# S4 convolution and MLP block on one core: the recorded order of 1,094 operations, the choice of engine and the PSUM slots replaced by another set

## The chip, the cores and the metric

One core of one Trainium2 chip runs the program. The core has five engines that work at the same time, each through its own list of instructions and strictly in that list's order: TensorE (PE in the profile; its weight loads are shown apart as PEld), VectorE (DVE), ScalarE (ACT), GpSimd (POOL) and SyncE (SP, which here only issues transfers). They meet through semaphores. Matmul results land in PSUM, which this kernel treats as eight slots (0 to 7) of 128 x 512 float32. The metric is the device time of one execution in microseconds (us).

## The reference

A layernorm, a long convolution whose kernel is a sum of 128 complex exponentials for each of 512 channels, a skip, then two layernorms, an MLP with GELU and another skip, on a 2048 x 512 input in bfloat16:

```python
def _A_ref(u, A_re, A_im, B_re, B_im, C_re, C_im, log_dt, Dskip):
    dt = jnp.exp(log_dt)[:, None]
    logdA = dt * (A_re + 1j * A_im)
    P = jnp.exp(logdA[:, :, None] * l[None, None, :])
    K = jnp.einsum("dn,dnl,dn->dl", Cc, P, dt * Bc).real
    ...
    return irfft(rfft(u, 2L) * rfft(K, 2L))[:L] + u * Dskip

def _B_ref(x, w1, b1, w2, b2):
    h = gelu(layernorm(x) @ w1 + b1)
    return h @ w2 + b2

h = x + _A_ref(layernorm(x), ...)
h2 = h + _B_ref(layernorm(h), ...)
```

## The kernel before

The program does not loop over tiles when it is built. It first writes down 1,094 operations, each with the engine or the two engines that may run it, what it reads and writes, and the PSUM slots that it needs. Then `Sched.run` goes through a recorded list, `ORDER`, and emits them in that order. An entry of 0 or more is twice the number of an operation, plus 1 if the second of its two engines is to run it; for a copy out of PSUM (`evac`) an even entry is ACT and an odd one DVE. A negative entry -1-z is a fill: one 128 x 128 x 512 matmul of the identity into the free slot z whose result nobody reads (L1434 in the profile). `SLOTS` says, digit by digit, in which slot each PSUM tile starts. An engine's own instructions are those of the list that belong to it, in the list's order, so `ORDER` sets each engine's queue, the order in which SP issues transfers, and with the slots who waits for whose PSUM tile. No time is computed when the program is built.

The 512 channels are handled in four blocks c = 0 to 3 of 128, in two halves (0 and 1, 2 and 3). The work around the change, in the order in which the data flow:

- Front (lines 560 to 760): small elementwise operations on DVE and ACT make rates, angles and sizes; 48 small transfers of 16 KB restack them (SP). `bexps` (L723) and `aexps` (PE L964, ACT L967) make the exponentials.
- `chain` (half; PE L992, ACT L1000, DVE L1010) and `chain1` (one block; PE L1024 and L1027, ACT L1029, DVE L1031): phases are added up in PSUM step by step, ACT takes the sine of each step, DVE multiplies it into the exponentials. The next step of a chain adds onto the PSUM tile that the sine reads, so it waits for that sine.
- `kgen` (block; PE L1054 and L1055, 512 pairs of narrow matmuls in all): the convolution kernel's table. It needs all five steps of the block's `chain1`. Operations 605 to 608, 610 and 611 are block 2, operations 628 to 634 block 3.
- `kspec` (blocks 0 and 1, L1084) and `kspec1` (block 2 or 3, L1109) put the table in order; it goes to DRAM (AK_d, AKc_d) and comes back transposed (KF). `fstage` (L940) is the second step of the transform; `austage` (L919) the first step for the input. `ktail` and `klate` (L1148, L1169) do the same for the late part. The copies out of PSUM of all of these are `evac` (ACT L517, DVE L519).
- The second half of the input's rows is loaded by eight transfers (`load_u(1)`), which wait for two tables made by ACT; DVE takes its statistics (L899) and normalises it (L906).
- `inverse` (DVE L1193, PE L1203): the products of spectra and the inverse transform, first for the first 1024 rows (operations 656 to 694), then for the others (846 to 897). Results are transposed by SP transfers (L1219), for block 3 of the first half on PE (L1212).
- `tail` (L1273, L1278 and the statistics of the layernorms) and `mlp` (PE L1321, ACT L1323 for the GELU, PE L1337, DVE L1339, output transfers). Operation 850 is the first matmul group of the inverse for the second 1024 rows; what PE has after it is the same in both orders but for the sequence.

Of the kernel before, what the change touches and what calls it, by code (L numbers as in the profile page):

```python
# [182 lines left out]
class VS(V):  # L183
# [60 lines left out]
SLOTS = "01012012034626026502020244602624062662062604046020262604064202462704264026024602460264206406204602467024602745020120415701425601624024672303642074350501246210675460165323401613712360172314231041502310"  # L244
# [5 lines left out]
class Sched:  # L250
# [44 lines left out]
    def run(self, nslots):  # L295
# [13 lines left out]
        taken = [None] * nslots  # L309
        given = iter(SLOTS)  # L310
        order, seen = [], set()
# [1174 lines left out]
```

## Time and profile before

| | |
|---|---|
| time, median of 3 runs | 245.29 us (243.12 to 245.49) |
| the profiled execution's own time | 245.59 us |
| its span in the profile | 243.2 us |
| PE busy | 215.4 us in 3,696 matmuls, 38 of them fills |
| DVE busy | 179.6 us in 407 instructions |
| ACT busy | 170.5 us in 232 instructions |
| transfers | 21.40 MB in 42,448 packets |

The span is the profile's time from the first to the last instruction; the difference of 2.4 us to the execution's own time lies around it. All engines run side by side, so busy times are no sum: in each stage the question is which queue is full, and what ended the last wait before it.

### The profile page before, as it was taken

How to read it: one execution, taken by the hardware profiler on the slowest of the kernel's cores; microseconds unless marked ns; L12 is line 12 of the kernel's file. 1: busy time of each engine (PE TensorE's matmuls, PEld its weight loads, DVE VectorE, ACT ScalarE, POOL GpSimd, SP SyncE). 2: the span in 40 equal slices, each digit the busy share in tenths (PEclk: the TensorE clock that was granted, in tenths of full speed). 3: DMA queues.
4: the chain of work that ended last, by engine and by line, in shares of the span. 5: the costliest groups of instructions: out<-in, count | busy, mean ns of one | idle time of the engine just before them, and what ended most of it. 6: DMA issues, size and time to landing. Idle time of an engine off the chain costs nothing.

```text
span 243.2 us, 8615 instructions
## 1 busy us (share of the span) xinstructions
PE 215.4 (89%) x3696; PEld 126.2 (52%) x3705; DVE 179.6 (74%) x407; ACT 170.5 (70%) x232; POOL 18.3 (8%) x145
## 2 busy tenths in 40 slices
PE   7559786878988876979998999999999999999994
PEld 2436243656634454755775476655554444444443
DVE  6999999999999995659998988797506991213022
ACT  3999999999999956975997987785134402903700
POOL 8800000011000000300000010010000101000000
PEclk9999999999999999999999999999999999999999
DMA  5121124000013943417899485644514051142303
GB/s 149 34 62 44 38 19 82 20 3 7 3 25 82 214 132 125 125 30 163 231 159 210 121 254 95 214 80 85 99 28 83 0 106 27 41 88 65 86 19 71
DMA packets 42448, 21.40 MB, mean 88 GB/s; under 512 B 30761, under 2 KB 40618, under 8 KB 42410
## 3 DMA queue, kind: packets, MB, share of 16 engines
q1 hardware_dynamic: 42250, 20.79, 38.0%
q8 instruction: 29, 0.48, 0.8%
q10 hardware_dynamic: 160, 0.07, 0.1%
q14 instruction: 9, 0.07, 0.1%
HBM read 10.33 MB, written 4.49 MB: 61 GB/s over the span
## 4 chain that ended last, share of the span: by engine, by line
PE 59%; DVE 26%; DMA 5%; issue 4%; SPq 3%; ACT 1%; DVEq 0%; ACTq 0%
PE ps L1321 16%; PE ps L1337 16%; PE ps L1203 7%; DVE ar L579 5%; DVE ar L519 4%; DMA ar<-ar 4%; PE ps L919 4%; PE ps L940 3%; DVE ar L1010 3%; SPq L530 3%; DVE ar L584 3%; PE ps L1054 3%; DVE ar L1031 3%; PE ps L1278 3%; PE ps L1055 2%
## 5 line engine op out<-in xcount | busy, mean ns | idle before, releaser
L517 ACT CAST ar<-ps 128x1024 bf16<-128x1024 f32 (+4 forms) x66 | 59.0, 941 | 16.7 <-PE ps L1203 7.5
L1323 ACT ACTIVATE ar<-ps,ar 128x512 bf16<-128x512 f32 (+1 forms) x44 | 27.6, 686 | 35.3 <-PE ps L1321 35.3
L1321 PE MATMUL ps<-ar 128*128 128x512 bf16 (+1 forms) x176 | 39.8, 379 | 0.0
L1337 PE MATMUL ps<-ar 128*128 128x512 bf16 (+2 forms) x179 | 38.5, 366 | 0.6 <-issue 0.3
L1339 DVE TENSOR_TENSOR ar<-ps,ar 128x512 bf16<-128x512 f32 (+1 forms) x17 | 10.8, 657 | 36.1 <-PE ps L1337 32.7
L519 DVE CAST ar<-ps 128x1024 bf16<-128x1024 f32 (+5 forms) x29 | 29.2, 1015 | 8.9 <-ACT ar L1029 2.8
L1193 DVE TENSOR_TENSOR ar<-ar 128x1024 bf16<-128x1024 bf16 x48 | 30.7, 685 | 6.5 <-PE ps L1203 6.0
L1337 PEld LDWEIGHTS <-ar 128*128 128x128 bf16 (+1 forms) x187 | 18.0, 98 | 19.6
L1321 PEld LDWEIGHTS <-ar 128*128 128x128 bf16 (+1 forms) x176 | 17.2, 100 | 20.4 <-issue 1.0
L1054 PE MATMUL ps<-ar 128*20 128x33 bf16 x512 | 20.0, 249 | 6.1 <-issue 5.6
L1203 PE MATMUL ps<-ar 64*128 64x128 bf16 x768 | 23.7, 216 | 0.1
L1203 PEld LDWEIGHTS <-ar 64*128 64x128 bf16 x768 | 21.5, 94 | 4.3 <-issue 2.1
L1029 ACT ACTIVATE ar<-ps 128x1024 bf16<-128x1024 int16 x20 | 19.6, 1039 | 3.0 <-issue 2.4
L579 POOL TENSOR_TENSOR ar<-ar 128x4 f32<-128x4 f32 (+1 forms) x6 | 7.4, 1226 | 187.5 <-DVE ar L584 149.3
L1010 DVE TENSOR_TENSOR ar<-ar 128x1024 bf16<-128x1024 bf16 x32 | 21.2, 684 | 0.2
L1055 PEld LDWEIGHTS <-ar 128*20 128x20 bf16 x512 | 17.7, 125 | 6.5 <-issue 6.4
L1055 PE MATMUL ps<-ar 128*20 128x33 bf16 x512 | 20.1, 248 | 0.0
L1054 PEld LDWEIGHTS <-ar 128*20 128x20 bf16 x512 | 17.6, 124 | 3.0 <-DVE ar L1031 1.5
L723 ACT ACTIVATE ar<-ar 128x512 bf16<-128x512 f32 x32 | 18.2, 628 | 0.5 <-DVE ar L565 0.5
L919 PE MATMUL ps<-ar 128*32 128x512 bf16 x256 | 15.7, 380 | 1.4 <-ACT ar L517 0.6
L1027 PE MATMUL ps<-ar 128*32 128x256 f16 (+2 forms) x288 | 13.5, 280 | 2.8 <-ACT ar L1029 2.7
L1031 DVE TENSOR_TENSOR ar<-ar 128x512 bf16<-128x512 bf16 x40 | 15.4, 413 | 0.3
(99 smaller groups left out, 284.6 us busy)
## 6 DMA issues: line engine op xcount, KB each, us to landing
ar<-in_A_u_dram SPq DMA_DIRECT2D x16, 128.0 KB
ar<-in_A_u_dram SPq DMA_DIRECT2D x8, 256.0 KB
out_dram<-ar SPq DMA_DIRECT2D x30, 64.0 KB
ar<-in_B_w_dram SPq DMA_DIRECT2D x4, 344.0 KB
ar<-in_B_w_dram SPq DMA_DIRECT2D x2, 640.0 KB
AK_d<-ar SPq DMA_DIRECT2D x2, 512.0 KB
ar<-AK_d SPq DMA_DIRECT2D x2, 512.0 KB
AKc_d<-ar SPq DMA_DIRECT2D x4, 256.0 KB
```

The lines of the kernel that those rows point to most:

```text
L517: act.copy(out_fn(), in_fn())
L519: dve.tensor_copy(out_fn(), in_fn())
L919: pe.matmul(pst(p)[32 * j:32 * j + 32, 512 * z:512 * z + 512], lhsT=BX.ap()[:, f0 + z, 16 - 16 * c:48 - 16 * c], rhs=src[2 * j + c].ap(), ...
L1010: add("DVE", c_dve(1024, 2), lambda e, lo=lo, rv=rv, sz=sc[z], e0=e0, o0=o0, q=q: dve.tensor_tensor(ent(o0, q, lo, 4, rv), ent(e0, q, lo, ...
L1031: add("DVE", c_dve(512, 2), lambda e, sc=sc, b0=b0, tb=tb, z=z: dve.tensor_tensor(tb[b0:b0 + 4].ap(), EA[c][b0:b0 + 4].ap(), sc[z].ap(), A ...
L1054: pe.matmul(o, lhsT=Ar.ap()[:, :, d], rhs=Br.ap()[:, :, d], start=True, stop=False, tile_position=(0, 32 * g))
L1055: pe.matmul(o, lhsT=Ai.ap()[:, :, d], rhs=Bi.ap()[:, :, d], start=False, stop=True, tile_position=(0, 32 * g))
L1193: dve.tensor_tensor(o, a, b_[:, :, ::-1, :] if sw else b_, ALU.mult)
L1203: pe.matmul(pst(p)[:, 512 * h + 128 * k:512 * h + 128 * k + 128], lhsT=q.ap()[rows, 2 * k + r, :], rhs=TP[w].ap()[rows, f0 // 2 + k, :], s ...
L1321: pe.matmul(pst(p)[:fs], lhsT=w1s[dc].ap()[:, fc * P:fc * P + fs], rhs=ybuf.ap().rearrange("p (t c) k -> p c t k", c=4)[:, dc], start=(dc ...
L1323: add("ACT", c_act(512, 1), lambda e, p=p, fc=fc, fs=fs: act.activation(hT.ap()[:fs, fc, :], pst(p)[:fs], ACT.Gelu_apprx_tanh, bias=b1_sb. ...
L1337: pe.matmul(pst(p)[:, c0:c1], lhsT=hT.ap()[:fs, fc, 128 * t:128 * t + 128], rhs=w2s[fc].ap()[:fs, c0:c1], start=(fc == 0), stop=(fc == NFC ...
```

## The change

The code stays as it is, line for line. `ORDER` and `SLOTS` are replaced. The same 1,094 operations are emitted; what differs:

- TensorE has 70 fills in place of 38. Between operation 532 (the first kgen group of block 0) and operation 605 (the first of block 2) there are 29 in place of 3; after operation 850 there are 9 in place of 10.
- Of the operations that either of ACT and DVE may run, 27 go from DVE to ACT and 24 from ACT to DVE, nearly all of them copies out of PSUM.
- PE: ahead of operation 605 it has six operations more: the austage group 422, the last three steps of chain1 for block 3 (494, 498, 502), the fstage group 572 and the small selection (530). In the old order these stand between the kgen groups of block 2 or later. Among the kgen groups of blocks 2 and 3 there now stand fstage groups and the two kspec1 groups of block 2.
- ACT: ahead of the last sine that kgen of block 2 needs (operation 483) seven copies and two sines (491, 495) come in, five copies go out. DVE: ahead of the last product that kgen of block 2 needs (485) seven copies and one product (496) come in, and two very small ones, five copies go out.
- SP: of the eight loads of the second half of the input, three stand ahead of the first AK_d write and one behind it; then a write of the late part, the second AK_d write, the other late write, the last four loads, and the two reads of AK_d. In the old order all eight loads stand ahead of both AK_d writes, with the two late writes among the two reads.
- The slots of most PSUM tiles differ.

The list's core around operation 605 (entry 1210):

```diff
 ORDER = [
...
-    770, 968, 970, 976, 774, 866, 863, 852, 1210, 982, 1212, 988, 854, 978, 844, 984, 760, 986, 990, 1214, 846, 996, 998, 1012, 772, 1114, 1140, 1142,
-    1014, 1106, 1216, 1004, 1218, 1024, 1020, 1220, 1026, 1006, 1016, 1022, 1160, 1000, 992, 1116, 1002, 1124, 1126, 994, 1144, 1163, 1222, 1120,
...
+    844, 864, 866, 972, 948, 784, 914, 840, 936, 974, 950, 980, 847, 944, 938, 946, 848, 956, 843, 982, 988, 856, 1208, 851, 958, 964, 952, 954, 960,
+    852, 990, 1106, 966, 859, 968, 996, 998, 1144, 962, 992, -1, -1, -1, 1004, 1006, 970, 1210, 1206, 774, 778, 780, 776, 1024, 1212, 1214, 854, 984,
...
 ]
-SLOTS = "01012012034626026502020244602624062662062604046020262604064202462704264026024602460264206406204602467024602745020120415701425601624024672303642074350501246210675460165323401613712360172314231041502310"
+SLOTS = "01201210213462462424024025260420620464646042402040460242640260424600002460426024204604202460260420462304206345600167246074120120462460230452362040615360730561047654354670170230124123145606567215210412"
```

More of the change, by code (lines that the diff above doesn't have):

```diff
@@ L199 @@
 ORDER = [
[43 rows of a table removed]
[44 rows of a table added]
 ]
-SLOTS = "01012012034626026502020244602624062662062604046020262604064202462704264026024602460264206406204602467024602745020120415701425601624024672303642074350501246210675460165323401613712360172314231041502310"
+SLOTS = "01201210213462462424024025260420620464646042402040460242640260424600002460426024604204602460260420462304206345600167246074120120462460230452362040615360730561047654354670170230124123145606567215210412"
 TURN = 450000
```

83 rows, old and new, of the table ORDER are left out of this document.

## The prediction

> **What bounds the kernel now.** I read the page first, for which engine is full in which part of the span.
>
> ```profile
> PE 215.4 (89%) x3696; PEld 126.2 (52%) x3705; DVE 179.6 (74%) x407; ACT 170.5 (70%) x232; POOL 18.3 (8%) x145
> PE   7559786878988876979998999999999999999994
> DVE  6999999999999995659998988797506991213022
> ACT  3999999999999956975997987785134402903700
> ```
>
> One slice is 6.1 us. For the first fifteen slices DVE and ACT are both full and PE is not; from slice 18 (about 109 us) PE is full to the end. The view of busy time by stretch, cut where PE starts the kgen groups of block 2 (85.2), kspec1 of block 3 (108.6) and operation 850 (139.06), says it in numbers:
>
> ```profile
> 46.00:62.00 16.00, 13.21 (x550) 10.78 (x547) 15.85 (x42) 15.97 (x28) 1.69 (x1) 1.00 0.03 7
> 62.00:85.20 23.20, 20.45 (x458) 10.84 (x456) 22.84 (x48) 23.18 (x28) 0.00 (x0) 1.00 0.42 86
> 85.20:108.60 23.40, 18.60 (x644) 13.92 (x644) 16.19 (x41) 17.07 (x20) 2.16 (x2) 1.00 0.36 106
> 108.60:139.06 30.46, 29.39 (x660) 18.51 (x662) 27.89 (x38) 25.91 (x30) 0.00 (x0) 1.00 0.81 171
> 139.06:239.90 100.84, 100.15 (x967) 53.94 (x973) 52.98 (x108) 47.34 (x69) 4.03 (x4) 1.00 0.39 87
> ```
>
> The columns are length, busy time of PE, PEld, DVE, ACT and POOL with instruction counts, granted clock, the transfers' share and GB/s. Up to 85.2 the two elementwise engines leave no gap (23.18 and 22.84 of 23.20). After 139.06 PE is busy for 100.15 of 100.84 us, and both orders have the same work there but for one fill. So the question is when operation 850 starts. The weak stretch is the third, where no engine is full: PE idles 4.8 of 23.4 us. The chain of waits names what it waited for:
>
> ```profile
> 82.50 0.44 PE ps L1027 x16
> 82.94 0.86 PE ps L919 x16
> 85.22 0.27 PE ps L1054 x4
> 85.48 0.07 PE ps L1055 x4
> ...
> 86.63 1.62 issue
> ...
> 91.13 0.55 PE ps L940 x4
> ...
> 92.34 1.83 issue
> ...
> 103.24 0.33 PE ps L1133 x4
> ...
> 105.72 1.01 issue
> ```
>
> "Issue" is a wait for nothing that the profile shows. The group of line 1054 in this stretch puts 4.5 us on it:
>
> ```profile
> L1054 PE MATMUL ps<-ar 128*20 128x33 bf16 x256 | 10.5, 249 | 4.5 <-issue 4.5
> ```
>
> These waits stand at fixed distances. Counted between the end of one and the start of the next:
>
> ```profile
> 46.70:50.20 3.50, 2.44 (x148) 2.32 (x137) 3.50 (x8) 3.49 (x9) 0.00 (x0) 1.00 0.05 10
> 88.20:92.30 4.10, 4.05 (x128) 2.81 (x128) 4.02 (x8) 3.00 (x4) 0.00 (x0) 1.00 0.71 200
> 94.10:105.60 11.50, 11.43 (x384) 8.69 (x384) 7.02 (x20) 10.06 (x12) 2.16 (x2) 1.00 0.29 85
> 106.70:130.50 23.80, 23.31 (x639) 16.51 (x638) 21.57 (x31) 17.98 (x22) 0.00 (x0) 1.00 0.80 161
> ```
>
> From 88.20 to 92.30 PE runs 128 matmuls and 128 loads, 256 instructions; from 94.10 to 105.60 it runs 768, three times 256; from 106.70 to the wait at 130.72 it runs 1,277, within the few records that a trace lacks five times 256. So PE stops where a block of 256 instructions ends and the next is not there. The view of transfers shows blocks on a queue of their own (q8, 16 KB a packet). Here are four windows: 82.1 to 85.7, 85.7 to 86.8, 86.8 to 91.8 and 91.8 to 93.
>
> ```profile
> q1 hardware_dynamic: 1909, 1.00, 115.6%
> ...
> q8 instruction: 1, 0.02, 5.2%
> ...
> q1 hardware_dynamic: 352, 0.63, 46.8%
> ...
> q8 instruction: 1, 0.02, 5.0%
> ```
>
> The first and third have no q8 packet at all: for 3.6 and 5.0 us the data queue had the engines, and PE's waits end at 88.25 and 94.17, 1.2 to 1.5 us after the windows that hold the next q8 packet. SP's own timeline says which data: eight input loads and two AK_d writes up to 81.6, then the AK_d reads.
>
> ```profile
> 74.05 1.87 SPq L530 DMA_DIRECT2D ar<-in_A_u_dram  x3
> 76.60 3.74 SPq L530 DMA_DIRECT2D ar<-in_A_u_dram  x5
> 80.44 1.16 SPq L530 DMA_DIRECT2D AK_d<-ar  x2
> 88.12 0.34 SPq L530 DMA_DIRECT2D ar<-AK_d  x1
> ```
>
> **A rule against the change.** The row: two waits of 1.62 and 1.83 us at block ends. The Trainium skill, Runtime: NRT & Kernel Launch, section on instruction fetch mechanics, states that instructions come in 16 KiB blocks of 256, fetched while the current one runs, and that crossing a block's end is mostly hidden. The trace agrees on the 256 and not on "hidden". By that rule the waits would have another cause, and spacing the instructions would save none of them; that is the second rival below.
>
> **The change part by part.**
>
> *The start of the kgen groups of block 2 moves later.* They need the last sine and product of that block's chain1. ACT has two sines and, net, two copies more ahead of that point; DVE net two copies and a product more. From the page:
>
> ```profile
> L517 ACT CAST ar<-ps 128x1024 bf16<-128x1024 f32 (+4 forms) x66 | 59.0, 941 | 16.7 <-PE ps L1203 7.5
> L519 DVE CAST ar<-ps 128x1024 bf16<-128x1024 f32 (+5 forms) x29 | 29.2, 1015 | 8.9 <-ACT ar L1029 2.8
> L1029 ACT ACTIVATE ar<-ps 128x1024 bf16<-128x1024 int16 x20 | 19.6, 1039 | 3.0 <-issue 2.4
> L1031 DVE TENSOR_TENSOR ar<-ar 128x512 bf16<-128x512 bf16 x40 | 15.4, 413 | 0.3
> ```
>
> Busy time by count is 0.98 per sine and 0.89 per copy on ACT, so 3.7 us; on DVE 1.01 per copy and 0.39 per product, so 2.4. Both queues were full, so nothing hides it. I take 3.3, near ACT's end since its window is the fuller, less something for two half-size copies: 88.5 in place of 85.2.
>
> *PE work is moved ahead of that start.* The austage group (0.86), three chain1 steps (0.44 each), an fstage group (0.55) and the selection (0.33) leave the stretch, 3.06 us. Four fills come in. The next rows are from the whole chain:
>
> ```profile
> 130.72 0.84 issue
> 141.36 2.26 PE ps L1434 x10
> ```
>
> A fill is 0.226 us, four are 0.9. Net -2.2 us. So the two first terms nearly cancel, and the gain has to come from the block waits.
>
> *The block waits.* Four kgen matmuls with their four loads take 0.07 us (the row at 85.48), so a block of nothing but kgen is used up in 256/8 x 0.07 = 2.2 us. With almost no transfers (the window 46.70 to 50.20, share 0.05) one block period took 3.5 us with PE idle for 1.06: that is the floor, and a wait of 1.3 us for a pure block. In the new order the run from 605 to the end of kgen of block 3 spans five blocks. The first is nearly pure (605 to 607) and the last about half as short (631 to 634 and four fills, 3.0 us); the middle ones hold thirteen fstage and kspec1 groups and last 3.8 us or more, over the floor. So at least 1.3 + 0.5 = 1.8 us stays. Whether more stays depends on transfers: the first AK_d write and half of the loads now go out earlier, and the AK_d reads no longer wait behind all eight loads, so they should be over when the run starts; but the loads of x for the tail (98 us in the old order) still fall into it. Bounds: 1.8 stay, or all 4.5. I take 2.3, near the floor: -2.2 us. Each block later has more work in it; of the wait at 130.72 I count half, -0.4, with 0 and -0.84 as its ends.
>
> *The second stretch and the end.* Copies that were deferred come back between 88 and 139. DVE, ACT and PE each have room there (16.2, 17.1 and 18.6 of 23.4 busy in the third window), so I cost them at nothing; if DVE fails to fit, its 2.4 us comes back. After 850 one fill less: -0.2. The table lookups and the front (two copies moved to ACT) are inside the first term, since ACT is counted from its start.
>
> Sum: +3.3 - 2.2 - 2.2 - 0.4 - 0.2 = -1.7. The profiled execution took 245.59 (span 243.2 and 2.4 around it), so 243.9. The median of the runs, 245.29, lies 0.3 below that execution, so 243.6.
>
> **The rivals.**
>
> *More is won.* The start moves by 2.4 only, the block waits fall to the floor (-2.7) and the one at 130.72 goes (-0.84): with -2.2 and -0.2 that is -3.5, and 241.8; less if the copies that waited for late sines (2.8 us in the L519 row) close up too, down to about 239. For it: no engine is full in the third window. Against it: DVE was busy for 27.89 of 30.46 in the fourth.
>
> *The waits stay as they are* (the rule above, or transfers that now meet the run in another place): +3.3 - 2.2 - 0.2 = +0.9, so 246.2. For it: a pure first block, requested just when the AK_d reads may still run. Against it: the 256-counts and the q8 packets.
>
> *Slower: PE becomes the bound ahead of the kgen run.* Between the first kgen groups and operation 605 PE gets 26 more fills (5.9 us) and the moved work (3.1), 9.0 us. It had idle time of 2.79 and 2.75 us in the first two windows, and the later start gives 3.3: 8.8. Nothing is left, while a step of a chain still has to wait for the sine ahead of it and holds up everything behind it on PE: the next step, and through it ACT and DVE. If all of the old idle time (5.5) was such waiting and is paid again, the time is 243.6 + 5.5 = 249.1. From 1.7 us of it on the kernel is slower than before, from 4.1 on by over 1%; I price it at 248. For it: the balance. Against it: a fill needs no data, so it can run early in a wait that is there anyway; then only its last 0.2 us can hold anything up.
>
> **How the numbers follow.** One per cent (2.45 us) is about what a measurement of this kernel tells from no change; the three runs differ by 2.4. Chances: the forecast (242.2 to 245.2) 0.42, more won 0.26, the waits stay 0.13, PE the bound 0.19. Faster by over 1% is under 242.84: 0.26 and 0.10 of the forecast's lower end, 0.36. Slower by over 1% is over 247.74: 0.17 of the last rival. The rest, 0.47, is within 1%. The range leaves out a tenth on each side: the far end of "more won" below 240.3 and PE as the bound in full above 248.3.
>
> **What would show it.** In the changed kernel's profile operation 605 should start near 88.5 us (first L1054 group of block 2) and 850 near 137.6 (the first L1203 group of 64 matmuls); the L1054 group should have 2 to 3 us on "issue" after 88 us, at distances of 256 instructions, and q8 packets no more than 1.5 us after a block's end. If ACT or DVE has gaps between 46 and 88 that end on PE L1027 or L992, PE has become the bound. If L1054 still has 4.5 us on issue, the spacing did nothing. If 850 starts before 136, the deferred copies cost less than I think.

## The result: 1.3 per cent slower, and the profile after

| | old order | new order |
|---|---|---|
| median of 18 runs each, side by side | 243.69 us (241.81 to 248.37) | 246.55 us (244.98 to 248.56) |
| ratio, 95% interval | | 1.0126 (1.0095 to 1.0158) |
| the profiled execution's own time, its span | 245.59 us, 243.2 | 245.81 us, 243.9 |

The ratio, here and below, compares runs of both orders made side by side and leaves out those more than 1.5 per cent above the fastest of their kernel, so it is not the quotient of the medians. The forecast was 243.6. The time is inside the range but on the other side of no change: a change of -1.7 us was forecast, and the medians differ by +2.9. The forecast started from 245.29, the median of three runs; the median of the 18 is 1.6 us lower. Note the table's last row: the two profiled executions differ by 0.2 us, the medians by 2.9. The execution of the old order that the prediction read was 1.9 us above the median of its kernel, that of the new order 0.7 below.

These are the page's rows for the new order (line numbers are one higher than in the old kernel):

```profile
PE 223.8 (92%) x3729; PEld 128.5 (53%) x3737; DVE 179.9 (74%) x404; ACT 171.7 (70%) x235; POOL 18.2 (7%) x145
...
PE   7559787989998999989999999999999999999993
...
DVE  6999999999899999778799889874525893003022
ACT  4899989989999979957789989695124516601900
...
L1055 PE MATMUL ps<-ar 128*20 128x33 bf16 x512 | 19.3, 249 | 1.1 <-issue 0.8
L1435 PE MATMUL ps<-ar 128*128 128x512 bf16 x70 | 18.0, 383 | 1.6 <-issue 1.2
```

PE has 8.4 us more of busy time, and 32 fills more (L1435, 18.0 us for 70, so 0.257 us each) are 8.2 of it. The kgen group L1055 (it was L1054) waits 0.8 us on issue. In the old profile it was 5.6 us, 4.5 of them in the kgen run of blocks 2 and 3:

```profile
L1054 PE MATMUL ps<-ar 128*20 128x33 bf16 x512 | 20.0, 249 | 6.1 <-issue 5.6
```

So most of the block waits of that profile are gone. The view of busy time by stretch says what was paid (columns as in the prediction; the borders are 605 at 91.33, 634 at 107.68 and 850 at 139.02):

```profile
46.00:62.00 16.00, 14.80 (x540) 11.24 (x538) 15.86 (x43) 15.05 (x26) 1.69 (x1) 1.00 0.10 12
62.00:75.00 13.00, 12.29 (x229) 5.64 (x231) 11.99 (x27) 12.97 (x16) 0.00 (x0) 1.00 0.06 12
75.00:91.33 16.33, 15.57 (x339) 8.46 (x331) 15.86 (x30) 14.75 (x18) 0.00 (x0) 1.00 0.85 205
91.33:107.68 16.35, 15.80 (x585) 12.61 (x585) 13.88 (x32) 13.99 (x16) 2.16 (x2) 1.00 0.31 78
107.68:139.02 31.34, 29.83 (x676) 18.33 (x668) 27.35 (x42) 25.38 (x30) 0.00 (x0) 1.00 0.88 186
139.02:240.04 101.02, 100.39 (x967) 53.72 (x972) 51.92 (x105) 48.93 (x72) 4.03 (x4) 1.00 0.38 77
```

In the first three rows PE idles only 2.7 of 45.3 us, and now ACT (15.05 of 16.00, 14.75 of 16.33) and DVE (11.99 of 13.00) have gaps that they did not have. Operation 605 starts 6.1 us later than in the old profile, not 3.3. The kgen run, from the start of 605 to the start of 634, is shorter, 16.35 in place of 21.53 us. Of the old order, the same view for that run and for what follows it:

```profile
85.22:106.75 21.53, 17.06 (x587) 12.79 (x589) 15.45 (x38) 16.68 (x19) 2.16 (x2) 1.00 0.39 114
106.75:139.06 32.31, 30.93 (x720) 19.64 (x721) 28.61 (x40) 26.27 (x31) 0.00 (x0) 1.00 0.77 162
```

Why 605 is late is read from the timeline of the new order (start and length in us):

```profile
51.73 1.02 PE L1435 MATMUL ps<-ar 128*128 128x512 bf16 x4 [1.17 <-issue]
52.69 0.62 PE L791 MATMUL ps<-ar 128*32 128x256 f16 x16
...
64.49 1.28 ACT L512 ACT_TABLE_LOAD   x1
...
65.64 1.32 DVE L520 CAST ar<-ps 128x726 bf16<-128x726 f32 x2 [0.61 <-PE ps L1056]
67.00 0.18 DVE L1069 TENSOR_TENSOR ar<-ar 128x32 bf16<-128x32 bf16 x1
67.09 0.88 DVE L585 SCALAR_TENSOR_TENSOR ar<-ar 128x256 f32<-128x256 f32 x2
...
69.11 5.85 SPq L531 DMA_DIRECT2D ar<-ar  x8
```

and of the old one:

```profile
61.82 1.28 ACT L511 ACT_TABLE_LOAD   x1
...
63.87 0.88 DVE L584 SCALAR_TENSOR_TENSOR ar<-ar 128x256 f32<-128x256 f32 x2
...
66.16 6.05 SPq L530 DMA_DIRECT2D ar<-ar  x8
```

This is one chain: the exponentials end, ACT loads the table for the sines (operation 357), ACT and DVE make the sizes for blocks 2 and 3 (358 to 363), SP restacks them in eight transfers, and only then does chain1 of block 2 start (466), five steps of which end in 605. In the new order five fills (the last four take 1.02 us) stand on PE ahead of the group at L791, and ACT waits 0.92 us for that group before it can copy its result out (operation 339, 53.36 us). This copy and a smaller one (104) were on DVE in the old order; now they stand in ACT's queue ahead of 357. On DVE two copies, the first of them after 0.61 us of waiting for PE, stand ahead of operation 359. Starts of the chain's members in several profiles, in us:

| operation | old, as read | old, 2nd profile | old, 3rd | new | new, 2nd | new, no fills | old, with fills |
|---|---|---|---|---|---|---|---|
| 357, table load (ACT) | 61.82 | 61.73 | 62.19 | 64.49 | 64.17 | 63.39 | 63.57 |
| restack (SP, first of 8) | 66.16 | 66.07 | 66.51 | 69.11 | 68.81 | 68.69 | 69.54 |
| 466, chain1 of block 2 | 73.19 | 73.09 | 73.63 | 76.49 | 76.08 | 76.48 | 77.28 |
| 483, its last sine | 83.06 | 82.96 | 83.41 | 88.23 | 87.92 | 87.61 | 86.83 |
| 485, its last product | 84.73 | 84.64 | 85.09 | 90.86 | 90.55 | 90.24 | 88.48 |
| 605, first kgen of block 2 | 85.22 | 85.12 | 85.57 | 91.33 | 91.03 | 90.71 | 88.96 |
| 634, last kgen of block 3 | 106.75 | 103.05 | 104.38 | 107.68 | 107.49 | 106.83 | 108.77 |
| 850 | 139.06 | 135.19 | 136.93 | 139.02 | 138.25 | 137.42 | 140.40 |
| run's own time | 245.59 | 241.39 | 243.40 | 245.81 | 245.13 | 244.23 | 247.46 |

### The profile page after: what moved, and what is told of

Same layout as the page of the kernel before. It is cut to its first block, busy times and chain, and to the rows that moved or that the text cites. A ratio compares the mean times of both kernels' runs of the same rounds, so it can differ in the third digit from the quotient of the medians.

```text
span 243.9 us, 8671 instructions
## 1 busy us (share of the span) xinstructions
PE 223.8 (92%) x3729; PEld 128.5 (53%) x3737; DVE 179.9 (74%) x404; ACT 171.7 (70%) x235; POOL 18.2 (7%) x145
## 4 chain that ended last, share of the span: by engine, by line
PE 63%; DVE 15%; ACT 13%; issue 4%; DMA 3%; SPq 0%; DVEq 0%; ACTq 0%
PE ps L1322 16%; PE ps L1338 15%; PE ps L1204 9%; DVE ar L1011 4%; ACT ar L518 4%; DVE ar L580 4%; PE ps L920 3%; PE ps L1435 3%; PE ps L941 3%; PE ps L1055 3%; ACT ar L1030 3%; PE ps L1279 2%; DVE ar L585 2%; PE ps L1056 2%; ACT ar L724 2%
## 5 line engine op out<-in xcount | busy, mean ns | idle before, releaser
L518 ACT CAST ar<-ps 128x1024 bf16<-128x1024 f32 (+3 forms) x66 | 58.5, 942 | 15.6 <-issue 4.9
L1194 DVE TENSOR_TENSOR ar<-ar 128x1024 bf16<-128x1024 bf16 x48 | 30.9, 686 | 8.5 <-PE ps L1204 6.7
L520 DVE CAST ar<-ps 128x1024 bf16<-128x1024 f32 (+4 forms) x29 | 29.0, 1013 | 7.2 <-issue 3.4
L1338 PEld LDWEIGHTS <-ar 128*128 128x128 bf16 (+1 forms) x187 | 18.1, 98 | 19.7
L1204 PE MATMUL ps<-ar 64*128 64x128 bf16 x768 | 24.2, 216 | 0.0
L1204 PEld LDWEIGHTS <-ar 64*128 64x128 bf16 x768 | 21.5, 94 | 4.7 <-issue 3.0
L1011 DVE TENSOR_TENSOR ar<-ar 128x1024 bf16<-128x1024 bf16 x32 | 20.3, 675 | 0.5 <-ACT ar L592 0.3
L1055 PE MATMUL ps<-ar 128*20 128x33 bf16 x512 | 19.3, 249 | 1.1 <-issue 0.8
L1435 PE MATMUL ps<-ar 128*128 128x512 bf16 x70 | 18.0, 383 | 1.6 <-issue 1.2
L1056 PE MATMUL ps<-ar 128*20 128x33 bf16 x512 | 19.3, 249 | 0.0
L1055 PEld LDWEIGHTS <-ar 128*20 128x20 bf16 x512 | 17.4, 124 | 3.4 <-issue 2.2
L1032 DVE TENSOR_TENSOR ar<-ar 128x512 bf16<-128x512 bf16 x40 | 15.9, 418 | 0.7 <-ACT ar L1030 0.3
```

The source lines that it names most:

```text
L518: act.copy(out_fn(), in_fn())
L520: dve.tensor_copy(out_fn(), in_fn())
L1011: add("DVE", c_dve(1024, 2), lambda e, lo=lo, rv=rv, sz=sc[z], e0=e0, o0=o0, q=q: dve.tensor_tensor(ent(o0, q, lo, 4, rv), ent(e0, q, lo, ...
L1055: pe.matmul(o, lhsT=Ar.ap()[:, :, d], rhs=Br.ap()[:, :, d], start=True, stop=False, tile_position=(0, 32 * g))
L1056: pe.matmul(o, lhsT=Ai.ap()[:, :, d], rhs=Bi.ap()[:, :, d], start=False, stop=True, tile_position=(0, 32 * g))
L1194: dve.tensor_tensor(o, a, b_[:, :, ::-1, :] if sw else b_, ALU.mult)
```

## The experiments

Times are medians; "ratio" is to the old order, run beside it on the same chip. Each diff shows the place that changed, taken out of longer lines of the list, and where several places change in the same way it shows one of them.

**before_again, before_third: the old order unchanged**, for other profiles of it.

> The kernel before, unchanged, profiled once more. Theory D (draw): the profiled execution of the kernel before that the prediction read, 245.59 us, was a slow draw; its median over 18 runs is 243.69. If its surplus of 1.9 us lay in the waits at the ends of instruction blocks, a second profile shows 1.5 to 2.5 us less on issue before line 1054 (it had 4.5) and operation 850 starts near 137 us in place of 139.06. Rival: the waits are the same in every execution (4.0 to 5.0 us), and the surplus lies elsewhere.

> The old order unchanged, a third profile. The landmarks up to 605 within 0.3 us of the first two (85.1 to 85.2); the run from 605 to 634 anywhere from 17.9 to 21.5 us, and operation 850 later or earlier with it (135.2 with the run of 17.9, 139.1 with 21.5). If it comes out near 18 again, the execution that the prediction read was the odd one.

242.54 us, ratio 0.9984 (0.9937 to 1.0031), and 243.20 us, ratio 0.9997 (0.9965 to 1.0029). The page's kgen group in the second and in the third profile:

```profile
L1054 PE MATMUL ps<-ar 128*20 128x33 bf16 x512 | 19.5, 249 | 2.3 <-issue 2.0
```

```profile
L1054 PE MATMUL ps<-ar 128*20 128x33 bf16 x512 | 19.6, 249 | 2.8 <-issue 2.3
```

The table's front is the same within 0.5 us in all three, but the run from 605 to 634 took 21.5, 17.9 and 18.8 us, and 850 came 3.9 and 2.1 us earlier than in the profile that the prediction read. Of these three the odd one was the first. The two pages count the kgen waits of the whole execution, 2.0 and 2.3 us on issue where the first profile has 5.6. In the run of blocks 2 and 3 alone, where the first profile has 4.5, they are 1.0 and 1.7. A fourth execution with the old list there (before_then_after, below) took 20.9 us for this run, with 2.3 on issue and a granted clock of 0.92 in it.

**after_again: the new order unchanged.**

> The new order unchanged, a second profile, and a second ratio beside 1.0126 (0.0031 either way). 605 within 0.3 us of 91.3, the run from 605 to 634 again 16.1 to 16.9 us (the new order has fewer waits at block ends, so it should vary less than the old one), 850 near 139; ratio 1.009 to 1.016.

245.68 us, ratio 1.0109 (1.0068 to 1.0149). Its kgen group:

```profile
L1055 PE MATMUL ps<-ar 128*20 128x33 bf16 x512 | 19.3, 249 | 0.8 <-issue 0.5
```

The run took 16.46 us, as in the first profile of the new order. The second measurement agrees with the first: slower by 1.1 to 1.3 per cent. This execution (0.6 us below its median) and the third of the old order (0.2 above) lie near their medians, so I use this pair below.

**after_nofill: the new order without its 29 fills between 532 and 605.** Seven places of the list change like this one, no operation moves:

```diff
-    828, 324, 602, -5, -5, -5, -5, -5, -5, -5, -5, 1082, 1084,
+    828, 324, 602, 1082, 1084,
```

> The changed order without the 29 fills between operations 532 and 605; nothing else is left out, and a fill computes nothing. Theory F (fills): they fill PE's queue (12.29 of 13.00 us busy at 62 to 75 in the changed kernel) and hold up the chain steps behind them, so operation 605 starts 2 to 5 us earlier than the 91.3 of the changed kernel and the time falls to 242 to 244.5. Rival: the fills lie in waits that are there anyway, 605 starts within 0.7 us of 91.3 and the time stays within 1 us of the changed kernel's 246.55; if the clock gate closes without them, it gets slower.

244.71 us, ratio 1.0039 (1.0004 to 1.0074). Against the two ratios of the new order, 1.0126 and 1.0109, the fills cost 0.7 to 0.9 per cent, 1.7 to 2.1 us, of the 2.9 or so that the new order loses; each of these ratios is uncertain by 0.8 to 1.0 us either way. In the stretches ahead of 605 its view of busy time reads

```profile
46.00:62.00 16.00, 12.13 (x526) 10.22 (x525) 15.86 (x44) 15.97 (x28) 1.70 (x1) 1.00 0.10 12
62.00:75.00 13.00, 11.09 (x229) 5.42 (x232) 12.09 (x27) 12.69 (x16) 0.00 (x0) 0.87 0.05 11
75.00:90.71 15.71, 13.80 (x321) 7.68 (x313) 15.53 (x29) 14.13 (x16) 0.00 (x0) 1.00 0.84 200
```

ACT is full again up to 62 us (15.97), and the table load comes 0.8 to 1.1 us earlier. The granted clock falls to 0.87 from 62 to 75, where it was 1.00 with fills. Even so the kernel is faster without them. But the theory was wrong about the way: 605 came only 0.3 to 0.6 us earlier, not 2 to 5, although PE now idles 7.7 of the 44.7 us ahead of it. Of the 0.9 and 1.5 us by which the span is shorter than in the two profiles of the new order, only these 0.3 and 0.6 lie ahead of 605; nearly all of the rest lies between 605 and 850. How the fills cost their full price is not shown.

**after_no_first_13_fills: only the first 13 of them left out** (the five behind operation 535, the eight behind 349).

```diff
-    1068, 1070, 682, -7, -7, -7, -7, -7, 676, 678,
+    1068, 1070, 682, 676, 678,
...
-    828, 324, 602, -5, -5, -5, -5, -5, -5, -5, -5, 1082, 1084,
+    828, 324, 602, 1082, 1084,
```

> The new order without the 13 fills that stand behind operations 535 and 349 (between 47 and 58 us); the other 16 ahead of 605 stay. Theory A (a fill costs where it holds up the exponentials of aexps and with them ACT's table load 357; in the profile without all 29 fills ACT was 1.0 us earlier from 56.9 us on): these 13 carry most of it, 357 starts at 63.4 to 63.7 in place of 64.5, and the time is 1.0 to 1.8 us below the new order, ratio to the old order 1.004 to 1.008. Rival (the fills behind 546 and 434, beside the first steps of chain, and the last ones carry it): 357 near 64.4, ratio 1.009 to 1.013.

245.54 us, ratio 1.0074 (1.0044 to 1.0104), between the two; 357 starts at 63.41, as early as without any fill. Both numbers lie where Theory A put them, and what the fills add to the delay of the table load is due to these 13. But the interval takes in almost nothing as well as almost all of the fills' price, so the time does not say which fills carry it. And 63.41 is still 1.2 us later than in the third profile of the old order, a delay that is there with none of the 29 fills too.

**before_with_fills: the mirror, 26 fills put into the old order** behind the same operations of PE, in place of its three.

```diff
-    820, 390, 698, 754, 824,
+    820, 390, 698, -4, -4, -4, -4, -4, -4, -4, -4, 754, 824,
```

> The old order and slots, with 26 fills in place of 3 between operations 532 and 605, behind the same operations of PE as in the new order. Theory A (the fills cost time, as leaving them out of the new order won 1.8 us): 23 fills are 5.2 us; half or less is hidden in the 5.5 us that PE is idle there, so 605 starts 0.5 to 2 us later than 85.2 and the time grows by 0.5 to 2 us, ratio 1.002 to 1.008. Rival (in the old order PE's idle time takes them, and they cost only where the other moved work has filled it): 605 within 0.3 us of 85.2, ratio 0.998 to 1.002.

247.00 us, ratio 1.0103 (1.0060 to 1.0147): above what I expected, 2.5 us (1.5 to 3.6) for 23 fills. The busy time ahead of 605 shows how:

```profile
46.00:62.00 16.00, 13.46 (x494) 10.36 (x495) 15.79 (x42) 14.54 (x25) 1.69 (x1) 1.00 0.03 8
62.00:75.00 13.00, 12.81 (x278) 6.34 (x276) 9.91 (x22) 11.54 (x15) 0.00 (x0) 1.00 0.04 9
```

From 62 to 75 PE is full (12.81 of 13.00) and the two engines that used to be full there, DVE and ACT, have 9.91 and 11.54. In this stretch the fills alone made PE the full engine, and 605 came 3.4 to 3.8 us later than in the three profiles without them.

**before_spaced_9: nine fills in the kgen run of the old order**, one behind each of nine kgen groups. It puts the prediction's idea of spacing to the test without moving anything.

```diff
-    1210, 982, 1212, 988, 854,
+    1210, 982, 1212, -7, 988, 854,
```

> The old order with nine fills more, one behind each of the kgen groups 606, 607, 608, 610, 611, 629, 630, 631 and 633. Nine fills are 2.0 us of PE. Spacing theory (PE waits for the next block of instructions anyway, so other work in the run is absorbed): the L1054 group's issue falls by 1 us or more against an execution of the old order, the run from 605 to 634 stays within 18 to 21.5 us, the ratio is 0.998 to 1.003. Rival (PE's work in the run is paid in full): ratio 1.006 to 1.010.

244.42 us, ratio 1.0067 (1.0036 to 1.0098): 1.6 us for 2.0 us of fills. In its timeline the first wait at a block's end is

```profile
88.02 0.27 PE L1055 MATMUL ps<-ar 128*20 128x33 bf16 x4 [0.52 <-issue]
```

where the third profile of the old order has

```profile
88.34 0.27 PE L1054 MATMUL ps<-ar 128*20 128x33 bf16 x4 [1.36 <-issue]
```

So work in the run does take the place of a wait, but there was little to take (1.0 and 1.7 us in the second and third profile), and by the time most of the fills' 2.0 us was paid.

**before_new_transfers: the old order with only SP's sequence changed**, the AK_d writes (1114, 1106) ahead of the last four loads and the reads (1118, 1116) ahead of the two late writes; run twice. The 14 entries in their old and their new sequence:

```diff
-    788, 776, 786, 780, 782, 778, 784, 774, 1114, 1106, 1116, 1206, 1118, 1208,
+    788, 786, 782, 1114, 784, 1106, 774, 778, 780, 776, 1118, 1116, 1208, 1206,
```

> The old order on PE, ACT and DVE; on SP alone the two AK_d writes move ahead of the last four of the eight loads of the second half, and the two AK_d reads stand right behind the loads, ahead of the two late writes. Theory D (the waits at the ends of instruction blocks in the kgen run depend on which transfers run then; the sequence of PE has little to do with it): the reads are out and over several us earlier, 605 stays at 85 us, the run from 605 to 634 takes 16.5 to 18.5 us in place of 17.9 to 21.5, the time falls by 0.5 to 3 us, ratio 0.988 to 0.998. Rival (the waits come from the run of 256 instructions itself, which is used up faster than the next block can come): the run takes 18 us or more as before and the ratio is 0.998 to 1.002. If the last loads land later and DVE's statistics (operation 506) wait for them, 506 starts later than 87.9 and the ratio is above 1.002.

> The same kernel as before_new_transfers once more, for a profile in which the clock is not held back and for the ratio. If the transfers' sequence wins what the first measurement showed, the ratio is 0.990 to 0.998 again, 605 starts near 85.3, the waits at block ends between 605 and 634 sum to 2 us or less, and 850 starts at 135 to 137. If the first measurement was chance, the ratio is 0.998 to 1.002.

243.24 us, ratio 0.9949 (0.9912 to 0.9986), then 242.39 us, ratio 0.9977 (0.9942 to 1.0012). SP's timeline in the second:

```profile
75.68 0.54 SPq L530 DMA_DIRECT2D AK_d<-ar  x1
...
78.33 0.52 SPq L530 DMA_DIRECT2D AK_d<-ar  x1
...
83.08 0.81 SPq L530 DMA_DIRECT2D ar<-AK_d  x2
```

The reads go out at 83.1 in place of 88.1, as meant. The run took 18.0 us, no less than the second profile of the old order. It is the fastest kernel of the study, by 0.2 to 0.5 per cent; the second interval takes in no change, so the gain is not certain.

**before_new_transfers_late_x: the same, and the three loads of the tail's input moved behind nine other transfers** (1390, 1392, 1394).

```diff
-    1654, 1226, 1228, 1390, 1042, 1054,
+    1654, 1226, 1228, 1042, 1054,
...
-    1188, 1190, 1280, 1168, 1170,
+    1188, 1190, 1280, 1390, 1392, 1394, 1168, 1170,
```

> As before_new_transfers, and the three loads of the tail's input (operations 695, 696, 697) move on SP behind the writes and loads that follow them (826 to 829, 617, 621, 644, 640), from about 96 us to about 108 us or later. Theory D (data transfers in flight delay the next block of instructions and PE stops for it): the kgen run has less traffic under it, the lags of the blocks requested between 91 and 106 us fall from 1.1 to 5.6 us to under 1.5, the run from 605 to 634 takes 16.5 to 18 us, the ratio is 0.984 to 0.995. Rival (the lag is moved, not removed: the same loads then delay the blocks between 110 and 125 us): the run is shorter by 1 us or more, but 850 starts no earlier than in before_new_transfers, and the ratio equals that of before_new_transfers within 0.3 per cent.

246.15 us, ratio 1.0157 (1.0112 to 1.0202). The run became no shorter (18.7 us), and the three loads now stood ahead of the AKc_d reads on SP; the view of PE's waits from 105 to 140 us shows a wait of 3.9 us that was not there:

```profile
PE ps L940 <- DMA ar<-AKc_d: 3.9, 1, 3.9
```

Neither theory had that. It tells nothing of the lags, only what a place in SP's queue is worth.

**after_old_transfers: the new order with the old sequence of the 14 transfers.**

```diff
-    788, 786, 782, 1114, 784, 1208, 1106, 1206, 774, 778, 780, 776, 1118, 1116,
+    788, 776, 786, 780, 782, 778, 784, 774, 1114, 1106, 1116, 1206, 1118, 1208,
```

> The new order with the old sequence of these 14 transfers on SP: all eight loads first, then the AK_d writes, the reads with the late writes among them. Theory D (that sequence of transfers removed the waits at block ends): the AK_d reads move 2 us or more later, under the kgen run that starts at 91.3; the L1055 group shows 2 us or more on issue in place of 0.8, fstage groups that need the reads (566, 568) come later, and the time grows by 0.7 to 3 us over the new order, ratio to the old order 1.015 to 1.025. Rival (the later start of the run alone took it out of the transfers' way): the same time as the new order, ratio 1.010 to 1.015.

245.41 us, ratio 1.0124 (1.0100 to 1.0148), that of the new order; the run took 16.5 us again. The sequence of transfers is not what shortened the run.

**after_block2_first: block 3's sines (982, 990), product (992) and steps (988, 996) behind those of block 2.**

```diff
-    848, 956, 843, 982, 988, 856, 1208, 851, 958, 964, 952, 954, 960, 852, 990, 1106, 966, 859, 968, 996, 998, 1144, 962, 992,
+    848, 956, 843, 856, 1208, 851, 958, 964, 952, 954, 960, 852, 1106, 966, 982, 988, 990, 996, 859, 968, 998, 1144, 962,
```

> The new order with five entries moved: the two sines of block 3 (operations 491 and 495) go behind the last sine of block 2 (483) on ACT, the product 496 behind 485 on DVE, the two chain1 steps that need them (494, 498) behind them on PE. Nothing else changes. Theory A (the kgen run starts late because ACT and DVE have more work queued ahead of it, and a later start is paid in full): two sines are 2.0 us and the product 0.4, so 483 starts about 2 us earlier than 88.2 and 605 about 2 to 2.4 earlier than 91.3, and the time falls by 1 to 2 us, ratio to the old order about 1.005. Rival B (the start of the kgen run is not what the end waits for; block 3's own chain is): 605 starts earlier, but 628 or 634 and 850 do not, and the time stays, ratio 1.01 or above. Rival C (the wait for the next block of instructions comes back since the run then meets the reads of AK_d): 605 earlier, the L1055 group with 2 us or more on issue.

250.75 us, ratio 1.0233 (1.0181 to 1.0284). The sine 483 started at 88.17 in place of 88.23: the two sines in front of it cost nothing. Without them ACT waits for PE instead, 1.15 us ahead of the sine 479 and 1.11 ahead of 483. And block 3's last step (502), which stands ahead of 605 on PE, then came at 95.2, and 605 at 95.7. The edit was a bad one, but it shows that the number of instructions ahead in ACT's queue is not the delay here, where the steps of two chains alternate.

**after_nofill_earlier_605: after_nofill with 605 freed sooner** (copy 429 to ACT, product 496, step 502 and sine 503 later).

```diff
-    852, 990, 1106, 966, 859, 968, 996, 998, 1144, 962, 992, 1004, 1006, 970, 1210, 1206, 774, 778, 780, 776, 1024, 1212, 1214,
+    852, 990, 1106, 966, 858, 968, 996, 998, 1144, 962, 970, 992, 1210, 1206, 774, 778, 780, 776, 1024, 1212, 1004, 1006, 1214,
```

> The new order without the 29 fills, and with four entries moved so that operation 605 can start sooner: the product 496 of block 3 goes behind 485 on DVE, the copy 429 from DVE to ACT behind the sine 483, and chain1's step 502 with its sine 503 behind the kgen group 606. Theory A (a microsecond of earlier start of the kgen run is a microsecond of time): 605 starts 0.8 to 1.5 us earlier than the 90.7 of after_nofill, and the time falls by 0.5 to 1.5 us, ratio 0.998 to 1.002. Rival (the kgen run then meets the reads and loads still under way until 91 us and waits for its next block of instructions, or block 3's step 502, moved back, holds 628): 605 earlier, but 634 and 850 not by as much, ratio 1.003 to 1.007.

245.48 us, ratio 1.0113 (1.0090 to 1.0136), slower than after_nofill. 605 started at 89.83, 0.9 earlier, but 634 at 107.94, 1.1 later. The step that had been done before the run now stood in it. So the instructions moved did hold 605 up by 0.9 us, but a start that was earlier by so much won nothing here. That the work left for PE behind it is the reason is my reading.

**after_old_engines: the new order, each of the 51 operations on its old engine** (the last bit of 51 entries).

```diff
-    866, 972, 948, 784, 914, 840, 936, 974, 950, 980, 847, 944, 938, 946, 848, 956, 843,
+    866, 972, 948, 784, 914, 840, 936, 974, 950, 980, 846, 944, 938, 946, 848, 956, 842,
```

> The new order, fills and slots, but each of the 51 operations that changed its engine (27 to ACT, 24 to DVE) runs on the engine it had in the old order. Theory A (ACT's and DVE's longer lists ahead of operation 605 make the late start): ahead of 357 ACT has 1.4 us less, ahead of 483 it has 5.1 us out and 4.6 in, so 0.5 less, DVE ahead of 485 about 1.7 less; 605 starts 1 to 1.5 us earlier, and the time falls by up to 1.5 us, ratio 1.006 to 1.012. Rival (the sequence itself, not the engine, costs the time, and the flipped choice was fitted to the sequence): with the old engines copies queue behind others, 605 no earlier and the time the same or up to 3 us longer, ratio 1.012 to 1.025.

271.15 us, ratio 1.1105 (1.1053 to 1.1158). The choice of engine fits the sequence and can't be exchanged by itself; the experiment says no more of the two.

**after_then_before, before_then_after: one order's list up to operation 850, the other's from there** (with other slots for some tiles).

```diff
 ORDER = [
...
-    1444, 1310, 1668, 1638, 1438, 1436, 1440, 1700, 1704, 1308, 1702, 1442, 1446, 1465, -7,
+    1444, 1310, 1668, 1638, 1438, 1436, 1440, 1410, 1396, 1308, 1678, 1404, 1700, 1702, 1706, 1710, 1442, 1446,
```

> The changed list up to operation 850 and the old list's order for all that is left after it (a few PSUM slots near the seam differ). Theory E (early): the 2.9 us between the medians are lost before operation 850, so this kernel is as slow as the changed one, 245.8 to 247. Theory L (late): they are lost after 850, so it is as fast as the old one, 243 to 244.5.

> The old list up to operation 850 and the new list's order for all that is left after it. Theory E (early): as fast as the old kernel, 243 to 244.5. Theory L (late): as slow as the changed one, 245.8 to 247. If both hybrids land in the middle, each half costs its share.

247.89 us, ratio 1.0171 (1.0112 to 1.0230), and 248.44 us, ratio 1.0184 (1.0106 to 1.0262). Both are slower than both parents. From 850 to the last product they take 103.5 and 104.5 us, the parents 100.8 and 101.0, so the seam itself costs 2.5 to 3.5 us and the halves can't be told apart in this way. Inconclusive.

## Why the prediction was wrong, step by step

**The step that failed first is "The start of the kgen groups of block 2 moves later", "I take 3.3".** It was 6.1 in the first pair of profiles and 5.5 in the second. The step took ACT's queue for the one that sets this start, and put the size near a count of ACT's work. That size was right for ACT; the busy time of each engine up to the sine 483 in the new order, in the old, and in the new order without fills is

```profile
0.00:88.23 88.23, 74.63 (x1471) 42.49 (x1475) 83.20 (x221) 81.32 (x116) 12.01 (x139) 1.00 0.28 61
```

```profile
0.00:83.06 83.06, 65.17 (x1396) 38.95 (x1400) 80.06 (x216) 78.05 (x113) 12.14 (x139) 1.00 0.23 49
```

```profile
0.00:87.61 87.61, 69.06 (x1447) 40.51 (x1451) 82.22 (x221) 81.32 (x117) 12.12 (x139) 0.98 0.28 59
```

ACT's busy time grew by 81.32 - 78.05 = 3.3 us, and its idle time by (88.23 - 81.32) - (83.06 - 78.05) = 1.9. The step left the idle time out. That PE was full is not the main reason for it: without the fills, with PE far from full, 1.3 of the 1.9 are still there. And it is half luck that 3.3 matched, since after_block2_first showed that two of the sines counted cost nothing.

What the operation 605 waits for in the end is the product 485, on DVE. Up to its start DVE's work was counted at 2.4 us and set aside as the smaller. The views up to 485, new and old:

```profile
0.00:90.86 90.86, 77.26 (x1512) 43.67 (x1515) 85.83 (x226) 83.37 (x118) 12.01 (x139) 1.00 0.30 68
```

```profile
0.00:84.73 84.73, 66.84 (x1424) 39.79 (x1428) 81.70 (x221) 79.72 (x114) 12.14 (x139) 1.00 0.25 54
```

DVE's busy time grew by 4.1 us, more than ACT's. One reason is the price: 1.01 per copy is the mean of a group of six shapes, and a 128x1024 copy, of which the new order has more there, takes 1.2:

```profile
85.33 2.34 DVE L520 CAST ar<-ps 128x1024 bf16<-128x1024 f32 x2
87.60 1.21 DVE L1032 TENSOR_TENSOR ar<-ar 128x512 bf16<-128x512 bf16 x3
88.72 1.22 DVE L520 CAST ar<-ps 128x1024 bf16<-128x1024 f32 x1
89.86 1.42 DVE L1032 TENSOR_TENSOR ar<-ar 128x512 bf16<-128x512 bf16 x4
```

These rows follow each other without a gap, and 605 starts at 91.33, right behind them. Without the fills DVE is the one engine without room in the last stretch (15.53 of 15.71 us busy, PE 13.80, ACT 14.13), and 605 comes at 90.71. That DVE holds up the last 0.9 us is shown by after_nofill_earlier_605: with the copy 429 and the product 496 out of its way, 485 started at 89.36 in place of 90.24. The rest is read from the table's starts, and no run takes it out: in the second pair 2.3 us of the 5.5 are there when the restack begins, 4.5 at the sine, 5.5 at the product.

**The rival "PE becomes the bound ahead of the kgen run" was the better reading of the fills, not of the start.** Its balance, 9.0 us more on PE against 8.8 us of room, came true: 42.66 of 45.33 us busy up to 605. What the prediction held against it ("a fill needs no data, so it can run early in a wait") is refuted: the fills do cost time, 1.7 to 2.1 us taken out of the new order and 2.5 put into the old one, by the ratios, and not the 5.5 of the rival's full price. But in the new order 605 is late with or without them. The rival "the waits stay as they are" is nearest in its number (246.2) by luck, since the waits went.

**"The block waits" was right in its mechanism and wrong in its size.** The waits fell to 0.8 and 0.5 us on issue, below the 1.8 that the prediction called the least, and the run to 16.1 to 16.5 us in six of the nine executions that have the new order's list there, some with an edit in it (16.7 to 18.1 in the others). But what there was to win was 1.0 and 1.7 us in the second and third profile of the old order, where the prediction had 4.5 from one execution. Their views in the pair near the medians, 605 to 634 and 634 to 850, old and new:

```profile
85.57:104.38 18.81, 17.05 (x588) 12.86 (x592) 15.36 (x38) 15.49 (x18) 2.17 (x2) 1.00 0.48 138
104.38:136.93 32.55, 31.38 (x730) 19.68 (x720) 28.63 (x40) 27.53 (x32) 0.00 (x0) 1.00 0.75 160
```

```profile
91.03:107.49 16.46, 15.87 (x584) 12.64 (x584) 13.98 (x32) 14.00 (x16) 2.17 (x2) 1.00 0.29 77
107.49:138.25 30.76, 30.08 (x676) 18.42 (x668) 27.27 (x42) 25.39 (x30) 0.00 (x0) 1.00 0.85 190
```

From 605 to 850 the time falls by 4.1 us: PE's busy time by 2.5, where the prediction had 2.2 of moved work, and its idle time by 1.7, where it had 2.6 (2.2 and 0.4). So behind the start the forecast of -4.8 was near. The two stretches are best taken together: three groups (564, 614 and 618) that stood behind 634 stand in the run in the new order.

The late start alone does not shorten the run: with fills the old order started it at 88.96, and it took 19.8 us. Nor does the sequence of transfers (18.0 and 16.5, as without it). What is left is PE's own sequence, which I could not put into the old order by itself; that it is the cause is argued, not shown. The rule of the Trainium skill weighed in the prediction (Runtime: NRT & Kernel Launch, instruction fetch mechanics: crossing a block's end is mostly hidden) comes nearer to the measurement than I gave it credit for. The traces have 2.0 and 2.3 us on issue at kgen in a whole execution of the old order (5.6 in the first): little but not none.

**"The second stretch",** for which the sum has -0.4, was better than that: from 634 to 850 the time fell by 1.0 in the first pair (32.31 to 31.34) and by 1.8 in the second (32.55 to 30.76). **"After 850", -0.2,** came out at +0.7 and +0.8 from 850 to the end of the span. I had taken what PE has there as the same but for one fill; the sequence differs, and I take it for what cost: the last two products of the output, in the third profile of the old order and in the second of the new,

```profile
236.60 0.42 DVE L1339 TENSOR_TENSOR ar<-ps,ar 128x256 bf16<-128x256 f32 x1 [0.57 <-PE ps L1337]
...
237.75 0.42 DVE L1339 TENSOR_TENSOR ar<-ps,ar 128x256 bf16<-128x256 f32 x1 [0.72 <-PE ps L1337]
```

```profile
238.56 0.42 DVE L1340 TENSOR_TENSOR ar<-ps,ar 128x256 bf16<-128x256 f32 x1 [1.00 <-PE ps L1338]
...
239.28 0.42 DVE L1340 TENSOR_TENSOR ar<-ps,ar 128x256 bf16<-128x256 f32 x1 [0.29 <-PE ps L1338]
```

are 0.7 us apart in place of 1.15, so the last but one output goes out closer to the last. Of the 0.8 us, 0.2 lie ahead of the last product and 0.6 behind it; that the closer outputs are the reason is argued, not shown.

**The sum, made again on the pair near the medians:** 605 later by 5.5, the run shorter by 2.4, up to 850 by 1.8, the end longer by 0.8: +2.1 us of span, 241.1 to 243.2. Against the forecast's terms (+3.3, -4.8, -0.2) the start is worth 2.2 us of the error, the stretch up to 850 0.7 and the end 1.0. From 46 us to 850 it can be read on PE alone:

```profile
46.00:136.93 90.93, 82.71 (x2314) 54.33 (x2313) 83.13 (x168) 82.49 (x103) 3.85 (x3) 1.00 0.48 108
```

```profile
46.00:138.25 92.25, 88.42 (x2342) 56.39 (x2342) 84.83 (x170) 82.09 (x103) 3.86 (x3) 1.00 0.52 117
```

PE's idle time fell from 8.2 to 3.8 us, so 4.4 were won; its busy time grew by 5.7, and that is where they went. What remains without the fills, ratio 1.0039, is that 605 is still 5.1 us later against a run and a stretch that are shorter by 2.7 and 2.0, with the end 0.8 longer. I did not take that remainder apart further, and its interval reaches down to 1.0004.

## What to carry to other kernels

A filler instruction needs room at its very place in the queue: 23 to 29 fills cost 1.7 to 2.5 us here, put in or taken out, though PE had 5.5 us of idle time in that part. When idle time and filler time are of one size, look at who waits for the instruction behind the filler. A late start is found by following the chain that leads to it (here exponentials, table load, some small operations, eight transfers, five steps, and at its end a product on DVE) and not by adding up the queue of one engine. A mean over a group of several shapes is no price for the shape that is moved. And a wait that one profile shows can be a draw: before it is counted as something to win, compare the profiled execution's own time with the median, and if it lies above, count on less.

## What was not expected of the hardware

How long PE waits at the end of a block of instructions differs between executions of one program. In the three profiles of the old order PE stopped at 86.6, 86.5 and 87.0 us, the same block's end. The next packet on q8 started at 91.9, 88.7 and 89.5 us, which is 5.3, 2.2 and 2.5 us after that. Up to there all three agree within 0.5 us. The run from 605 to 634 then took 21.5, 17.9 and 18.8 us, and the runs of the old order in this study lie between 241.3 and 248.4 us.
